# Seven block products in place of eight in four split-float32 matmuls, with a Prelu sign step and an Identity scale step

## The chip, the cores and the metric

The kernel runs on one core of a Trainium2 chip. The metric is device time in microseconds (us) of one execution. Before the change the median of three runs is 1053.89 us (1053.65 to 1054.04).

The core's engines run side by side and wait for each other by semaphores: TensorE multiplies (PE in the profile, its weight loads PEld), VectorE (DVE) and ScalarE (ACT) work element by element, SyncE (SP) issues the DMA transfers here, and GpSimd (POOL) does nothing of note.

## The reference

Attention with a sigmoid in place of a softmax, then two feed-forward blocks. Four large matmuls follow the attention; `w_in` is 768x2048 and `w_out` 2048x768 in each block.

```python
def _attn_ref(q, k, v):                        # q, k, v: (4, 12, 448, 64)
    scores = scale * np.matmul(q, k.transpose(0, 1, 3, 2)) - np.log(S)
    attn = 1.0 / (1.0 + np.exp(-scores))
    return np.matmul(attn, v).astype(np.float32)

def _moe_ref(x, w_in, w_out, s, b):            # x: (1792, 768)
    r = np.maximum(x @ w_in, 0.0)
    return ((s * (r * r) + b) @ w_out).astype(np.float32)

def _moe2_ref(x, w_in, w_out, alpha):
    h = x @ w_in
    return ((np.maximum(h, 0.0) + alpha * np.minimum(h, 0.0)) @ w_out).astype(np.float32)
```

The weights `w_in` and `w_out` arrive as float64, since numpy promotes them when they are scaled; the kernel gets their bits and makes float32 of them on the chip.

## The kernel before, in words

Activations are kept transposed, channels on the 128 partitions and tokens along the free dimension.

**Precision.** Every float32 operand of the four large matmuls is split in two: `hi`, rounded by a cast (ACT, L99 and L210, or DVE, L212), and `lo = x - hi` (DVE, L102 and L217). A product of two 128-wide blocks is then three matmuls into one PSUM bank, hi x lo, hi x hi and lo x hi (L411 to L413), each with a weight load of its own.

**Attention** (`emit_qk`, `emit_sig`, `emit_av`, `emit_x`). There are 84 steps. Step u issues the score matmuls of step u (L281) and the value matmuls of step u-2 (L307), both on 64x64 quarters of the array with 448 columns; ACT takes the sigmoid out of PSUM (L291), and a finished head pair is added up by ACT (L318) and DVE (L319). Beside this the 16 `w_in` units of block 1 are converted.

**The four matmuls** (`PASSES`, `in_mm`, `out_mm`). Three token groups, of 768, 512 and 512 tokens, go one after the other through block 1 and then through block 2, so there are six passes of 16 input units (`w_in`, six k blocks each) and 18 output units (`w_out`, three cuts for each of six output blocks). In the 768 group, `products` merges part of the work (L416) and does the rest as 256-column matmuls (L402). `in_evac` takes a unit's result from PSUM and applies relu, square, scale and offset (L437 to L454) or the two-sided slope (L461 to L472); `out_evac` copies the result and stores it.

**Weights.** A float64 unit is loaded (`load64`, L127), converted by `convert` in four steps (sign, L141 on ACT or L143 on DVE; exponent, L147; low bits, L152; joined, L155), stored as float32 (L165) and loaded again in later passes (`load32`, L174); `split_unit` makes hi and lo of it two units ahead of its use.

**Order.** Tile pools with two to four buffers for each kind of tile, PSUM in four double banks (`acc`, `av`); the order of the instructions on each engine is the order in which the Python loops issue them. The last unit of all is cut in two halves of 256 tokens (L494 to L507), so that the last copy and store are short.

Of the kernel before, what the change touches and what calls it, by code (L numbers as in the profile page):

```python
# [21 lines left out]
NWARM = 6  # L22

@with_exitstack
def tile_kernel(
# [19 lines left out]
    DM = NK * P  # L57
    NFC = w_in1.shape[0]
    QKSCALE = 1.0 / math.sqrt(D)
    WMAX = NK * P  # L60
    T2 = 2 * S

    REST = B * S - 3 * N5
    TG = N5 + REST
    TOK = [TG, N5, N5]
    TOK0 = [0, TG, TG + N5]
    NCUT = len(OUT_CUTS)
    PER = NFC + NK * NCUT

    def pool(name, bufs, **kw):  # L70
        return ctx.enter_context(tc.tile_pool(name=name, bufs=bufs, **kw))

    const = pool("const", 1)
    xp = pool("xp", 1)
    gp = pool("gp", 1)
    r64p = pool("r64", 2)
    cvp = pool("cvp", 1)
    wrawp = pool("wraw", 4)
    whlp = pool("whl", 4)
    tp = pool("tp", 4)  # L80
    ps = pool("ps", 2, space=PSUM)
    ps_av = pool("ps_av", 2, space=PSUM)
    dram = pool("dram", 1, space=DRAM)

    def acc_tile(name):
        return ps.tile([P, 2, 512], F32, tag="acc", name=name)

    def av_tile(name):
        return ps_av.tile([P, 2, 512], F32, tag="av", name=name)

    def t_tile(name):
        return tp.tile([P, TG], F32, tag="t", name=name)

    def g_tile(fc, name="g"):
        return gp.tile([P, WMAX + T2], F32, tag=f"g{fc}", name=f"{name}{fc}")

    def split(hi, lo, src, eng_hi):
        if eng_hi == "A":
            nc.scalar.copy(hi, src)  # L99
        else:  # L100
            nc.vector.tensor_copy(hi, src)
        nc.vector.tensor_tensor(out=lo, in0=src, in1=hi.bitcast(F32), op=ALU.subtract)  # L102

    bias_t = const.tile([P, 1], F32, name="bias_t")
    s_t = const.tile([P, 1], F32, name="s_t")
    b_t = const.tile([P, 1], F32, name="b_t")
    warm = const.tile([P, 1], F32, name="warm")
    al_t = const.tile([P, NFC], F32, name="al_t")
    nal_t = const.tile([P, NFC], F32, name="nal_t")


    units = []
    for wi, wo in ((w_in1, w_out1), (w_in2, w_out2)):
        for fc in range(NFC):
            units.append((wi[fc], WMAX))
# [519 lines left out]
```

## Time and profile before

| | before |
|---|---|
| median of 3 runs | 1053.89 us (1053.65 to 1054.04) |
| span of the profiled execution, first to last instruction | 1052.1 us |
| PE busy | 1047.9 us |
| DVE busy | 594.8 us |
| ACT busy | 448.5 us |
| moved by DMA | 173.17 MB |

The profiled execution's own time is its span, 1052.1 us, and what lies around it; 1.8 us separate it from the median of the runs. "Busy" of an engine is the share of the span in which at least one instruction of it runs. A matmul's duration in the trace is its way through the array, and the next one starts before it ends, so the pace of matmuls is read from their starts and not from their durations. In the chain of work that ended last, pieces have a start and a length, and the length of a run of matmuls is the time until the next piece.

### The profile page before, as it was taken

The page shows a single profiled execution, that of the slowest core. Times are in us where ns is not written, and L with a number is a line of the kernel's source. Part 1 is how long each engine was busy: PE and PEld are TensorE (multiplying, and loading weights), DVE is VectorE, ACT ScalarE, POOL GpSimd, SP SyncE. Part 2 cuts the span into 40 slices and gives each one's busy share as a digit, 9 for nine tenths or more (in the row PEclk, how much of TensorE's full clock was granted, in tenths as well). Part 3 has the DMA queues.
Part 4 walks back from the last instruction along what each step waited for, and adds up shares of the span by engine and source line. Part 5 has one row for each costly group of instructions (what it writes and reads, how often), then busy time and mean ns, then how long its engine had stood idle before and what let it go on. Part 6 is the DMA issues. An engine that isn't in the chain of part 4 may idle for free.

```text
span 1052.1 us, 14275 instructions
## 1 busy us (share of the span) xinstructions
PE 1047.9 (100%) x5631; PEld 818.3 (78%) x5631; DVE 594.8 (57%) x881; ACT 448.5 (43%) x625; POOL 0.2 (0%) x4
## 2 busy tenths in 40 slices
PE   9999999999999999999999999999999999999998
PEld 4333388888888888888888888888888888888887
DVE  4765456687643775447745366786616652266521
ACT  6777733444332554335534333443314432344321
POOL 0000000000000000000000000000000000000000
PEclk9999999999999999999999999999999999999999
DMA  7787660048762545764566512468523235323330
GB/s 276 274 268 248 244 249 1 27 140 262 250 225 93 195 138 203 270 207 136 183 220 207 187 61 60 120 187 291 201 93 105 89 122 170 130 90 98 116 117 31
DMA packets 62131, 173.17 MB, mean 165 GB/s; under 512 B 8048, under 2 KB 10736, under 8 KB 62064
## 3 DMA queue, kind: packets, MB, share of 16 engines
q1 hardware_dynamic: 62064, 172.27, 49.1%
q8 instruction: 44, 0.72, 0.3%
q14 instruction: 23, 0.19, 0.1%
HBM read 132.92 MB, written 39.32 MB: 164 GB/s over the span
## 4 chain that ended last, share of the span: by engine, by line
PE 100%; DVE 0%; issue 0%; DVEq 0%
PE hps L411 12%; PE hps L412 12%; PE hps L413 12%; PE ops L411 12%; PE ops L413 12%; PE ops L412 12%; PE sc L281 6%; PE av L307 6%; PE ops L416 4%; PE hps L416 4%; PE hps L402 2%; PE ops L402 2%; PE ops L494 0%; PE wp L345 0%; DVE o L503 0%
## 5 line engine op out<-in xcount | busy, mean ns | idle before, releaser
L102 DVE TENSOR_TENSOR whl<-wraw,whl 128x768 fp32r<-128x768 f32 (+1 forms) x188 | 167.8, 903 | 130.8 <-ACT whl L99 130.1
L411 PE MATMUL hps<-x,whl 128*128 128x512 f32 x576 | 224.4, 390 | 0.0
L412 PE MATMUL hps<-x,whl 128*128 128x512 f32 x576 | 224.3, 389 | 0.0
L413 PE MATMUL hps<-x,whl 128*128 128x512 f32 x576 | 224.1, 389 | 0.0
L411 PE MATMUL ops<-g,whl 128*128 128x512 f32 x571 | 222.4, 389 | 0.0
L412 PE MATMUL ops<-g,whl 128*128 128x512 f32 x571 | 222.3, 389 | 0.0
L413 PE MATMUL ops<-g,whl 128*128 128x512 f32 x571 | 222.1, 389 | 0.0
L99 ACT CAST whl<-wraw 128x768 fp32r<-128x768 f32 (+1 forms) x188 | 146.7, 792 | 40.8 <-PE ops L413 25.5
L411 PEld LDWEIGHTS hps<-x,whl 128*128 128x128 f32 x576 | 108.2, 188 | 22.7 <-issue 0.7
L413 PEld LDWEIGHTS hps<-x,whl 128*128 128x128 f32 x576 | 108.1, 188 | 22.6
L412 PEld LDWEIGHTS hps<-x,whl 128*128 128x128 f32 x576 | 108.2, 188 | 21.8
L413 PEld LDWEIGHTS ops<-g,whl 128*128 128x128 f32 x571 | 107.2, 188 | 22.4
L412 PEld LDWEIGHTS ops<-g,whl 128*128 128x128 f32 x571 | 107.2, 188 | 21.7
L411 PEld LDWEIGHTS ops<-g,whl 128*128 128x128 f32 x571 | 107.2, 188 | 21.7
L291 ACT ACTIVATE ga<-sc,bias_t 128x896 f32<-128x896 f32 x84 | 84.5, 1008 | 33.2 <-PE sc L281 31.5
L217 DVE TENSOR_TENSOR g<-t,g 128x512 fp32r<-128x512 f32 (+1 forms) x128 | 77.2, 624 | 31.8 <-ACT g L210 28.6
L437 ACT COPY o<-ops 128x512 f32<-128x512 f32 (+1 forms) x35 | 23.1, 661 | 149.0 <-PE ops L413 92.1
L281 PE MATMUL sc<-ga 64*64 64x448 f32 x672 | 78.3, 544 | 0.0
L307 PE MATMUL av<-ga,ga 64*64 64x448 f32 x672 | 77.1, 536 | 0.0
L147 DVE SCALAR_TENSOR_TENSOR cva<-r,cva 128x768 f32<-128x768 f32 (+1 forms) x68 | 61.7, 908 | 6.0 <-ACT cva L141 4.7
L210 ACT CAST g<-t 128x768 fp32r<-128x768 f32 x32 | 26.7, 836 | 85.8 <-DVE t L465 42.0
L217 DVE TENSOR_TENSOR x<-xr,x 128x512 fp32r<-128x512 f32 (+1 forms) x36 | 22.7, 645 | 59.0 <-ACT x L210 59.0
(53 smaller groups left out, 817.3 us busy)
## 6 DMA issues: line engine op xcount, KB each, us to landing
wraw<-w SPq DMA_DIRECT2D x104, 384.0 KB, 3.1
r<-in_w_in SPq DMA_DIRECT2D x32, 768.0 KB, 5.1
r<-in_w_out SPq DMA_DIRECT2D x24, 640.0 KB, 5.1
wraw<-w SPq DMA_DIRECT2D x48, 320.0 KB, 3.5
ga<-in_qk SPq DMA_DIRECT2D x23, 448.0 KB, 5.2
r<-in_w_out SPq DMA_DIRECT2D x12, 768.0 KB, 5.4
w<-wraw SPq DMA_DIRECT2D x24, 320.0 KB, 5.7
ga<-in_vt SPq DMA_DIRECT2D x24, 256.0 KB, 5.3
```

The lines of the kernel that those rows point to most:

```text
L99: nc.scalar.copy(hi, src)
L102: nc.vector.tensor_tensor(out=lo, in0=src, in1=hi.bitcast(F32), op=ALU.subtract)
L147: nc.vector.scalar_tensor_tensor(out=a.bitcast(F32), in0=hi.bitcast(F32), scalar=2.0**-112, in1=a.bitcast(F32), op0=ALU.mult, op1=ALU.max,)
L217: nc.vector.tensor_tensor(out=lo[:, a - o : e - o], in0=src[:, a - c0 : e - c0], in1=hi[:, a - c0 : e - c0].bitcast(F32), op=ALU.subtract,)
L281: nc.tensor.matmul(sc[h * D : (h + 1) * D, j, :S], kqt[q][rows, S + k0 : S + k0 + D], kqt[q][rows, :S], start=True, stop=True,)
L291: nc.scalar.activation(sg, sct.pop(u)[:, :, :S], AF.Sigmoid, bias=bias_t[:, 0:1], scale=QKSCALE)
L307: nc.tensor.matmul(avt[q][j * D : (j + 1) * D, h, :S], vtt[q][keys, j, c, :], sg[keys, j, :], start=first, stop=last,)
L402: nc.tensor.matmul(dst[:, N5:TG], lo, mv[:, 2 * N5 : N5 + TG], start=start and k == 0, stop=stop and k == n, skip_group_check=True,)
L411: nc.tensor.matmul(dst[:, :N5], hi, mv[:, N5 : 2 * N5], start=first and k == 0, stop=False)
L412: nc.tensor.matmul(dst[:, :N5], hi, mv[:, :N5], start=False, stop=False)
L413: nc.tensor.matmul(dst[:, :N5], lo, mv[:, N5 : 2 * N5], start=False, stop=end)
L416: nc.tensor.matmul(dst[:, N5 : 2 * N5], hi, mv[:, 2 * N5 :], start=first and not short_first and k == 0, stop=last and short_first and k == n,
```

## The change

Each of the four matmuls is cut into blocks of two by two and done with seven block products in place of eight (Strassen's method in Winograd's form: M1 to M7). The left operands are blocks of the weights or sums of them (A11, A12, A22, S1 to S4), the right ones blocks of the activations or differences, and the results are sums of products. In particular:

- Tokens are cut in four groups of 448 (S); two of them make one 2x2 cut. The six passes become four phases, (block, token half), each with an `in_phase` (eight pairs of unit rows x seven products x three k blocks x three matmuls) and an `out_phase` (seven products x three output pairs x eight k blocks x three matmuls). Every matmul has 448 columns.
- `quad` converts two float64 units at a time: ScalarE's Prelu does the sign and exponent steps in one instruction, two DVE steps do the low bits, four DVE additions make S1 to S4, and one DMA stores all seven left operands in DRAM. There are 34 quads, 20 in or right after the attention, 9 behind phase 0 and 5 behind phase 1 in program order. The buffers of the conversion (`R64` for two rows, `CVA`, `QUAD`) are single, and share their place with `XRAW[1]`.
- `unit` loads 1024 columns of left operands and splits them into a ring of three; 42 units in a phase.
- `make_x` forms the seven right operands of an input matmul (four differences, seven splits of 1344 columns); `prepare` does the same for an output matmul, one product ahead (four differences, seven splits of 3584 columns in three chunks).
- Results are added up while leaving PSUM (`pcopy` on ACT, `padd` and `psub` on DVE). M2, M4 and M7 accumulate in the bank that M1, M5 and M6 wrote, after that bank has been read.
- Scale and offset become an ACT Identity with scale and offset from SBUF; relu, square and Identity run on ACT for four blocks at a time.
- Nothing is issued as the loops run: every operation goes into a `Plan` with a written duration and what it reads and writes. `Plan.order` keeps PE's order, and picks for every other engine what can start first, then what is due first by the written durations. The kernel is issued in that order.
- PSUM is one tile of eight banks, SBUF is placed by hand.

```diff
...
-OUT_CUTS = [(0, 6), (6, 11), (11, 16)]
...
-PASSES = [(0, 0), (0, 1), (0, 2), (1, 0), (1, 1), (1, 2)]
-N5 = 512
...
+IN_ORDER = ["M1", "M5", "M6", "M2", "M7", "M4", "M3"]
+OUT_ORDER = ["M1", "M5", "M2", "M6", "M7", "M4", "M3"]
+LEFT = {"M1": "A11", "M2": "A12", "M3": "S4", "M4": "A22", "M5": "S1", "M6": "S2", "M7": "S3"}
+CHUNKS = [(0, 3), (3, 6), (6, 8)]
...
+class Plan:
...
+                if eng == "PE":
+                    i = pe[pe_at]
...
+                    pick = (max(f, est[i]), late[i], i)
+                else:
+                    pick = min((max(f, est[i]), late[i], i) for i in cand)
...
+    NSLOT = 37
+    NRING, NRAW, NTMP = 3, 2, 8
+    UNIT = 8 * P
+    WQ = KH * P
...
+    RING = [tensor(f"ring{i}", RING0 + i * 2 * UNIT, 2 * UNIT, F32R) for i in range(NRING)]
+    XRAW = {0: tensor("xraw0", RING0, 4 * XB), 1: tensor("xraw1", PROD, 4 * XB)}
+    R64 = [tensor(f"r64{i}", PROD + 4 * WQ * i, 4 * WQ) for i in range(2)]
+    CVA = tensor("cva", PROD + 8 * WQ, 2 * WQ)
+    QUAD = tensor("quad", PROD + 10 * WQ, 7 * WQ)
...
+    ps = psp.tile([P, 8, 512], F32, name="ps")
...
+    def quad(m, kind, k, c):
...
+        for row in range(2):
...
+            load(raw, src.bitcast(U32), 4 * n, (), cells(r64, 4 * n))
...
+                nc.scalar.activation(a, hi, AF.Prelu, scale=2.0**-112, alpha=-(2.0**32))
...
+                nc.vector.tensor_scalar(
+                    out=u, in0=lo, scalar1=2.0**-29, scalar2=7.0, op0=ALU.mult, op1=ALU.min
...
+                nc.vector.scalar_tensor_tensor(
+                    out=u, in0=a.bitcast(U32), scalar=3, in1=u,
...
+        tt("S1", "S3", "A22", ALU.add)
+        tt("S3", "A11", "S3", ALU.subtract)
+        tt("S2", "S1", "A11", ALU.subtract)
+        tt("S4", "A12", "S2", ALU.subtract)
...
+            "SP", dma_t(7 * n), lambda: nc.sync.dma_start(out=dst, in_=src),
...
+    def unit(m, kind, i):
...
+        raw, dst = RAW[g % NRAW], RING[g % NRING]
...
+        split(dst, dst + UNIT, raw, UNIT)
...
+    def make_x(par, raw):
...
+        half(0, p[0])
+        minus(p[0], p[1], p[0], XB)
+        half(1, p[0])
+        minus(p[0], p[3], p[0], XB)
+        half(2, p[0])
+        half(3, p[2])
+        minus(p[1], p[3], p[1], XB)
+        half(4, p[1])
+        minus(p[0], p[0], p[2], XB)
+        half(5, p[0])
+        half(6, p[3])
...
+    def mm_group(dst_bank, terms, first, last, more=False):
...
+                nc.tensor.matmul(d, wh_, ml_, start=first and k == 0, stop=False, **opt)
+                nc.tensor.matmul(d, wh_, mh_, start=False, stop=False, **opt)
+                nc.tensor.matmul(d, wl_, mh_, start=False, stop=last and k == n, **opt)
...
+    def nonlinear(m, par, mp, ps_):
...
+            add("ACT", act_t(n), lambda: nc.scalar.activation(h, h, AF.Relu), c, c)
+            add("ACT", act_t(n), lambda: nc.scalar.activation(h, h, AF.Square), c, c)
...
+                lambda: nc.scalar.activation(h, h, AF.Identity, bias=b_t, scale=s_t),
...
+    def in_phase(m, par):
...
+        for mp in range(NMP):
+            k0 = 4 * (mp % 2)
+            a, c, bb, e = k0, k0 + 1, k0 + 2, k0 + 3
+            to = {"M1": a, "M2": a, "M5": c, "M4": c, "M6": bb, "M7": bb, "M3": e}
+            second = {"M2", "M4", "M7"}
+            for i, x in enumerate(IN_ORDER):
...
+                if x == "M1":
+                    t = tmp()
+                    pcopy(t, a)
+                elif x == "M5":
+                    s_ = tmp()
+                    padd(s_, c, t)
...
+                elif x == "M6":
+                    q = tmp()
+                    padd(q, bb, s_)
+                elif x == "M2":
+                    pcopy(g_place(par, 0, mp), a)
...
+                elif x == "M7":
+                    padd(g_place(par, 3, mp), bb, s_)
...
+                elif x == "M4":
+                    psub(g_place(par, 2, mp), g_place(par, 3, mp), c)
...
+                else:
+                    padd(g_place(par, 1, mp), e, q)
...
+    def out_phase(m, g, par, middle):
...
+            "M1": (P1, None), "M5": (P1, (P2, P1)), "M2": (P3, None), "M6": (P1, (P4, P1)),
+            "M7": (P2, (P4, P2)), "M4": (P1, (P1, P3)), "M3": (P4, None),
...
+        prepare(0)
+        for i, x in enumerate(OUT_ORDER):
+            if i + 1 < 7:
+                prepare(i + 1)
+            if i in middle:
+                middle[i]()
+            for k in range(NDP):
+                unit(m, "out", i * NDP + k)
...
+    quads = []
+    for m in range(2):
+        quads += [(m, "in", k, 0) for k in range(NMP)]
+        quads += [(m, "out", k, c) for c in range(len(CHUNKS)) for k in range(NDP)]
...
+        if u == 4:
+            produce(20)
...
+    phases = [(0, 0), (0, 1), (1, 0), (1, 1)]
+    for n, (m, g) in enumerate(phases):
+        par = n % 2
+        in_phase(m, par)
...
+            def early(nxt=nxt):
+                load_x(*nxt)
+                make_x(1 - par, 1)
+
+            middle[6] = early
+        out_phase(m, g, par, middle)
+        if n == 0:
+            produce(9)
+        if n == 1:
+            produce(len(quads))
+    plan.emit()
```

## Rows read from the trace of the kernel before

**Rows 1.** Page, parts 1 and 2: PE's busy time; clock and DMA by slice.

```profile
PE 1047.9 (100%) x5631; PEld 818.3 (78%) x5631; DVE 594.8 (57%) x881; ACT 448.5 (43%) x625; POOL 0.2 (0%) x4
...
PEclk9999999999999999999999999999999999999999
DMA  7787660048762545764566512468523235323330
```

**Rows 2.** Page, part 4: the chain that ended last, by engine.

```profile
PE 100%; DVE 0%; issue 0%; DVEq 0%
```

**Rows 3.** Chain in order of time: start us, length us, what.

```profile
142.62 1.36 PE hps L416 x6
148.06 1.36 PE hps L416 x6
149.42 1.43 PE hps L402 x12
154.96 1.36 PE hps L416 x6
...
1045.40 3.60 PE ops L494 x30
```

**Rows 4.** Stretches: bounds: length, busy PE, PEld, DVE, ACT, POOL; clock, DMA share, GB/s.

```profile
0.00:131.40 131.40, 130.35 (x1393) 50.87 (x1393) 72.94 (x121) 97.09 (x111) 0.20 (x4) 1.00 0.75 262
...
330.50:461.00 130.50, 130.50 (x577) 108.06 (x576) 77.61 (x112) 57.14 (x88) 0.00 (x0) 1.00 0.58 195
...
660.00:710.00 50.00, 50.00 (x243) 42.29 (x242) 42.61 (x66) 23.27 (x31) 0.00 (x0) 1.00 0.54 160
```

**Rows 5.** Groups by form on PEld: busy us, mean ns | idle before.

```profile
L411 PEld LDWEIGHTS hps<-x,whl 128*128 128x128 f32 x576 | 108.2, 188 | 22.7 <-issue 0.7
...
L402 PEld LDWEIGHTS hps<-x,whl 128*128 128x128 f32 x192 | 25.1, 191 | 1.2
```

**Rows 6.** Groups by form on DVE: busy us, mean ns, idle before, releaser.

```profile
L102 DVE TENSOR_TENSOR whl<-wraw,whl 128x768 fp32r<-128x768 f32 x116 | 110.4, 952 | 30.3 <-ACT whl L99 30.2
...
L147 DVE SCALAR_TENSOR_TENSOR cva<-r,cva 128x768 f32<-128x768 f32 x44 | 42.0, 955 | 3.7 <-ACT cva L141 2.6
...
L319 DVE TENSOR_TENSOR xo<-av,xo 128x448 f32<-128x448 f32 x24 | 15.0, 624 | 39.9 <-ACT xo L318 39.9
...
L439 DVE TENSOR_TENSOR t<-hps,t 128x256 f32<-128x256 f32 x32 | 13.5, 423 | 34.5 <-ACT t L437 34.5
...
L152 DVE TENSOR_SCALAR cw<-r 128x768 uint32<-128x768 uint32 x16 | 8.9, 554 | 0.0
```

**Rows 7.** Groups by form on ACT, same columns.

```profile
L99 ACT CAST whl<-wraw 128x768 fp32r<-128x768 f32 x116 | 96.3, 831 | 14.0 <-PE ops L416 7.9 <-PE ops L413 4.3 <-DMA wraw<-w 1.7
L291 ACT ACTIVATE ga<-sc,bias_t 128x896 f32<-128x896 f32 x84 | 84.5, 1008 | 33.2 <-PE sc L281 31.5
...
L437 ACT COPY t<-hps 128x768 f32<-128x768 f32 x32 | 25.5, 798 | 43.6 <-PE hps L402 25.7 <-PE hps L416 16.2 <-issue 1.7
...
L141 ACT ACTIVATE cva<-r 128x768 f32<-128x768 f32 x28 | 25.5, 910 | 11.8 <-DVE wraw L155 6.5 <-DMA r<-in_w_out 5.2
...
L318 ACT COPY xo<-av 128x448 f32<-128x448 f32 x24 | 12.6, 524 | 0.5 <-PE av L307 0.5
...
L352 ACT ACT_TABLE_LOAD x1 | 1.3, 1283 | 0.7 <-PEq L625 0.7
```

**Rows 8.** Three stretches of 10 us, columns as in rows 4.

```profile
30.00:40.00 10.00, 10.00 (x112) 3.81 (x108) 5.70 (x10) 7.80 (x9) 0.00 (x0) 1.00 0.91 333
...
70.00:80.00 10.00, 10.00 (x112) 3.84 (x108) 5.61 (x10) 7.37 (x10) 0.00 (x0) 1.00 0.95 322
...
140.00:150.00 10.00, 10.00 (x49) 8.40 (x48) 6.61 (x11) 3.95 (x5) 0.00 (x0) 1.00 1.01 394
```

**Rows 9.** Page, part 6, DMA issues: count, KB each, us to landing.

```profile
wraw<-w SPq DMA_DIRECT2D x104, 384.0 KB, 3.1
r<-in_w_in SPq DMA_DIRECT2D x32, 768.0 KB, 5.1
```

More of the change, by code (lines that the diff above doesn't have):

```diff
@@ new lines, in tile_kernel, with split @@
+    n_unit = [0]
+    ring = {}
+    def unit(m, kind, i):
+        g = n_unit[0]
+        n_unit[0] += 1
+        raw, dst = RAW[g % NRAW], RING[g % NRING]
+        load(
+            sb(raw, UNIT), w32[m, kind][:, i * UNIT : (i + 1) * UNIT], UNIT,
+            [("d", m, kind, 8 * i + j) for j in range(8)], cells(raw, UNIT),
+        )
+        split(dst, dst + UNIT, raw, UNIT)
+        ring[m, kind, i] = dst
+    def split(hi, lo, src, n):
+        h, l, x = sb(hi, n), sb(lo, n), sb(src, n)
+        add("ACT", act_t(n), lambda: nc.scalar.copy(h, x), cells(src, n), cells(hi, n))
+        add(
+            "DVE", dve_t(n),
+            lambda: nc.vector.tensor_tensor(
+                out=l, in0=x, in1=h.bitcast(F32), op=ALU.subtract
+            ),
+            cells(src, n) + cells(hi, n), cells(lo, n),
+        )
@@ new lines, in minus, with slots @@
+    def minus(o, x, y, n):
+        o_, x_, y_ = sb(o, n), sb(x, n), sb(y, n)
+        add(
+            "DVE", dve_t(n),
+            lambda: nc.vector.tensor_tensor(out=o_, in0=x_, in1=y_, op=ALU.subtract),
+            cells(x, n) + cells(y, n), cells(o, n),
+        )
+    def slots(name, par, k, n, dtype=F32R):
+        if par:
+            k = NSLOT - k - n
+        return tensor(name, SLOTS + k * SLOT, n * SLOT, dtype)
+    X = [[slots(f"xo{p}{i}", p, 3 * i, 3) for i in range(7)] for p in range(2)]
@@ new lines, in make_x, with half, load_x @@
+    def make_x(par, raw):
+        p = [XRAW[raw] + i * XB for i in range(4)]
+        pl = X[par]
+        def half(i, src):
+            split(pl[i], pl[i] + XB, src, XB)
+        half(0, p[0])
[9 more added lines that the diff above has]
+        half(6, p[3])
+    def load_x(m, g):
+        for i in (0, 1, 3, 2):
+            to = XRAW[1] + i * XB
+            load(
+                sb(to, XB), x_dram[m, g][:, i * XB : (i + 1) * XB], XB,
+                [("x", m, g, i, j) for j in range(KH)], cells(to, XB),
+            )
@@ new lines, in pcopy, with f, padd @@
+    def pcopy(dst, k, func=None):
+        d = sb(dst, S)
+        def f():
+            if func is None:
+                nc.scalar.copy(d, bank(k))
+            else:
+                nc.scalar.activation(d, bank(k), func)
+        add("ACT", act_t(S, True), f, [("p", k)], cells(dst, S))
+    def padd(dst, k, other):
+        d, o = sb(dst, S), sb(other, S)
+        add(
+            "DVE", dve_t(S, True),
+            lambda: nc.vector.tensor_tensor(out=d, in0=bank(k), in1=o, op=ALU.add),
+            [("p", k)] + cells(other, S), cells(dst, S),
+        )
@@ L331, in flush_stores @@
-    def flush_stores():
-        for dst, t in stores:
-            nc.sync.dma_start(out=dst, in_=t)
-        stores.clear()
+        k = avt.pop(q)
+        kh, i = divmod(pr, KH)
+        o = (2 * kh + bb % 2) * XB + i * S
+        t = XRAW[0] + o if bb < 2 else tmp()
+        pcopy(t, k)
+        padd(t, k + 1, t)
+        if bb >= 2:
+            store(x_dram[0, 1][:, o : o + S], t, [("x", 0, 1, 2 * kh + bb % 2, i)])
+            free(t)
     ctx.enter_context(tc.manual_schedule())
-    idle = const.tile([P, P], F32, name="idle")
+    idle = sb(IDLE, P)
```

824 lines of the change are left out of this document (423 added, 401 removed).

## The prediction

> **What bounds the kernel now.** I read the page's busy times first, then the chain that ended last, then the chain piece by piece, then the stretches. PE is busy for 1047.9 of 1052.1 us at full clock in all forty slices [rows 1], and the chain is 100% PE [rows 2]. The reader should see that nothing but the number and pace of matmuls sets the time; DVE (594.8 us) and ACT (448.5 us) are covers with room in them. Busy PE time doesn't give the pace, so I take it from starts. In the 768 group 5.44 us lie between 142.62 and 148.06 [rows 3], for 24 matmuls of 512 columns: 0.2267 us each. A pass of 576 such matmuls agrees (130.5 us) [rows 4]. Thirty matmuls of 256 columns take 3.60 us [rows 3]: 0.120 us each.
>
> **The sum is built on three stretches.** Attention ends at 131.4 us [rows 4]. From there to 1049.0 (1045.40 + 3.60) [rows 3] PE works off 3840 matmuls of 512 and 384 of 256 columns. 3840 x 0.2267 + 384 x 0.120 = 916.6 us, and 131.4 + 916.6 = 1048.0, so the pace explains the trace to 1 us. The last 3.1 us are copy and store. The median lies 1.8 us above this execution's span; I add 1.8 again.
>
> **PE after.** A phase has 504 + 504 matmuls, four phases 4032, all of 448 columns. That form isn't in the trace. Between 256 and 512 columns the pace rises by 0.1067 us in 256, so 448 columns take 0.2267 - 64 x 0.000417 = 0.2000 us, and all of them 806.4 us instead of 916.6. From below: if nothing in a matmul is fixed, 0.2267 x 7/8 = 0.1984, 6.5 us less in all. From above: with 256-column matmuls at 0.1217 (12.34 us for two units at 142.62 and 154.96, less 48 x 0.2267, over 12) [rows 3], 0.2005, 2 us more; that a 448 column matmul costs as much as one of 512 is a rival below. I take 0.2000, the interpolation. The attention's matmuls are unchanged (131.4), and the tail still is one addition and a store of 128 rows (3.1). Floor: 131.4 + 806.4 + 3.1 + 1.8 = **942.7 us**.
> The row has 13.4 ns on each matmul above 512 columns at 2.4 GHz. The Trainium skill (TensorE: Matmul & The Clock Gate, Back-to-back issue gap) gives 2.5 ns of fixed cost, 189.2 ns at 448 columns; by it the products would take 763 us and the sum be 899. Its figure for 512 columns, 215.8 ns, differs from the measured 226.7, so I don't follow it.
>
> **DVE and ACT after.** DVE instructions on PSUM take 0.423 us (256) and 0.624 (448), so 0.155 + 1.047 ns a column, which gives 0.959 at 768 where SBUF rows have 0.952 [rows 6]. ACT takes 0.524 (448) and 0.798 (768), 0.831 from SBUF [rows 7], 0.86 ns a column.
> - Quads: two rows of 0.554 + 0.955, four additions of 0.557: 5.25 us DVE for 28, 3.9 for the six narrower: 170. Prelu replaces L141 and L147; L141's strided read took 0.910 [rows 7], I take the same: 59 us ACT. If Prelu were as fast as a plain cast it gains 0.08 each, 5 us of a covered engine.
> - Units: 168 x 1.227 = 206 DVE, 168 x 1.05 = 176 ACT.
> - `make_x`: 4 x 11 x 1.562 = 69 DVE, 37 ACT. `prepare`: 44 x 4.217 = 186 DVE, 100 ACT.
> - Results: 160 + 60 + 24 additions of 0.624 = 152 DVE, the slope step 35. ACT: copies 46, block 1's three steps 85, block 2's two relus 60. Identity with two operands from SBUF has no row; the sigmoid with one took 1.008 at 896 columns against 0.91 on the copies' line [rows 7], so 0.1 each, 0.2 for Identity (0 to 0.4, times 16, all on ACT).
>
> Together DVE 818 us and ACT 661 with the attention's 97 [rows 4]. Both stay below 943, but DVE's room is gone: phase 0 asks 206 us of it (in 51, out 81, `make_x` 17, quads 56) in 202 of PE, phase 1 196, phase 2 189, phase 3 150. In a full queue instructions start before the previous ends (DVE's groups add to 622 us where 594.8 are busy), so the true shares are 4 to 8% lower.
>
> **What can hold PE**, each from both sides:
> - Attention. ACT has 131.4 - 97.1 = 34 us free [rows 4]. Eight or nine quads bring 15, `make_x` 9, first units 3. A Prelu of 0.9 us in front of a sigmoid delays it by less than the two steps that PSUM covers, unless it waits for its DMA; behind it on ACT stand the sigmoids, and PE waits for them. 0 to 10 us, I take 3.
> - The first `out_phase`. It needs 17 quads. By its start at 131.4 + 100.8 = 232 us, DMA has to move q, k, v 17.3 MB, x 2.8, 17 quads 47.2 and 24 units 12.6: 79.8 MB. The fullest stretches moved 322 at share 0.95, 333 at 0.91 and 394 at 1.01 GB/s [rows 8], so 339 to 390 when full: 205 to 235 us. And `QUAD` is single: a quad's chain is 5.6 us of DVE and ACT and then a 1344 KB store of 3.5 to 4.1 us plus 2.0 (384 KB land in 3.1 [rows 9], 1.1 of it bytes), 11.4 us alone, some 14 beside the attention's loads, 14.5 beside a half busy DVE. That is 8.5 quads by 131.4, and the other 8.5 (three narrow ones at 10.5) by 242; the last is due at 236. 0 (at 11.4 each) to 25 us (at 17), I take 7.
> - Collisions on DVE. M7 adds to the bank that M6's result leaves by DVE, with only M2 between (nine matmuls, 1.8 us). If DVE has just begun a unit's split, 1.2 + 0.6 + a handover fill the 1.8: 32 times 0 to 0.4, and up to 12 more where phases 0 and 1 ask all of DVE. 0 to 25, I take 5.
> - Six changes between in and out. `make_x` needs 17 us of DVE within two products that leave 14, but later planes are due 1.8 us apart. 0 to 2 each, I take 3.
>
> What is removed beside PE's work (`convert`'s extra steps, the casts of six passes) was covered and gives nothing of its own; all transfers together grow from 173 MB to some 220, most of it unit loads, which after the first phase have room. Sum: 942.7 + 3 + 7 + 5 + 3 = **961 us** (960.7).
>
> **Rivals.**
> 1. The conversion holds PE. If a quad takes 17 us throughout, the attention loses its 10, the first `out_phase` 25, phase 1 with nine more quads 5, and the collisions stay: 942.7 + 40 + 5 = 988. For it: the single `QUAD`, the DMA share it asks for. Against: 394 GB/s were reached. Decides at some 14 us a quad.
> 2. DVE becomes the bound. From 131.4 on it has 741 us of work. Its highest share over 50 us so far is 42.6 of 50, 85% [rows 4]; at that share 872 us, and 131.4 + 872 + 4.9 = 1008. Against: it then had nothing more to do.
> 3. Prelu isn't in the sigmoid's table. One table load of 1.283 us served sigmoid, copy, relu and square [rows 7]; no row shows Prelu or Identity. If each Prelu among the sigmoids cost two loads, 34 x 1.283 = 44 us would join ACT's 124 in the attention: 37 over, 942.7 + 37 + 15 = 995. The Trainium skill (ScalarE: Activation LUTs, Table sets: the hidden batching unit) says cheap functions, relu, copy and identity among them, are in every set, and speaks of 2.7 us for a switch; the trace agrees for relu and copy, and no row shows Prelu.
> 4. The weight load sets the pace: 188 ns and a gap of 39 each [rows 5], so 0.2267 stays: 131.4 + 914 + 4.9 = 1050. Against: at 256 columns the load has 191 ns too and the pace is 0.120.
> 5. Slower than before. PSUM is one tile; if its results can't leave while PE writes another bank, each of 308 results (224 in, 84 out) stops PE for 0.624 us [rows 6]: 192 us, 1135. It decides from 178 of them on (111 us, the difference from floor to before). Nothing in the trace shows it; the banks alternate, which speaks against it.
>
> **How the numbers follow.** The forecast (943 to 975) gets 0.62, the rivals 0.16, 0.10, 0.03, 0.04 and 0.05. The range 943 to 1000 takes in the forecast with nearly all its bounds, rival 1 and rival 3: 0.81. About 0.2% is what a measurement of this kernel can tell from no change. Faster by more: 0.62 + 0.16 + 0.10 + 0.03 and half of rival 4, 0.93; within 0.2% the other half, 0.02; slower 0.05.
>
> **What would show it.** 448-column matmuls 0.200 us apart, at full clock. Attention's end near 134; a gap in PE, if any, at the first product of the first `out_phase`, ended by a unit whose load waited for a quad's store. In phases 0 to 2 DVE above 85% busy; M7's first matmul waiting for DVE in some row pairs. One table load. Wrong would be: a pace above 0.205, more than one table load, gaps at every product, or DVE with idle time while PE waits for it. A granted clock below 1.00 behind a gap would add to every stall above.

## The result and the profile after

The changed kernel takes 1024.46 us (median of four runs, 1022.11 to 1028.94) against 1053.79 for the one before: a ratio of 0.9727, 95% interval 0.9702 to 0.9752. It is faster by 29 us, where 93 were forecast: 961 was predicted, 943 to 1000 the range. The profiled execution has a span of 1020.9 us.

The page of the changed kernel, parts 1 and 2 (busy us, share and count; clock and DMA by slice), beside [rows 1]:

```profile
PE 972.0 (95%) x5424; PEld 828.7 (81%) x5424; DVE 762.6 (75%) x896; ACT 625.8 (61%) x675; POOL 0.2 (0%) x4
...
PEclk9999999998899999999999989998999999999999
DMA  8998999886776657776579568765444533333441
```

The chain that ended last, by engine, beside [rows 2]:

```profile
PE 62%; DVE 11%; DMA 6%; ACT 3%; issue 3%; SPq 0%; DVEq 0%; ACTq 0%
```

Before, the chain was 100% PE. Now PE stands still for 49 us, DVE and DMA have links in the chain, and the granted clock is below 0.9 in four slices. Where that lies is read from the stretches. The first row is the attention, then come the four phases, each an `in_phase` and an `out_phase` of 504 matmuls (columns as in [rows 4]):

```profile
0.00:134.00 134.00, 130.96 (x1392) 61.24 (x1392) 71.09 (x101) 115.02 (x134) 0.20 (x4) 1.00 0.90 323
134.00:248.10 114.10, 105.74 (x509) 95.55 (x505) 85.70 (x125) 81.05 (x82) 0.00 (x0) 0.98 0.86 296
248.10:369.40 121.30, 110.15 (x505) 98.54 (x506) 102.56 (x110) 61.25 (x65) 0.00 (x0) 0.93 0.66 226
369.40:481.70 112.30, 104.75 (x505) 95.61 (x504) 79.06 (x107) 77.71 (x75) 0.00 (x0) 0.98 0.74 254
481.70:591.70 110.00, 104.51 (x505) 95.71 (x505) 95.00 (x102) 59.25 (x63) 0.00 (x0) 0.98 0.69 227
591.70:710.20 118.50, 108.87 (x506) 98.46 (x505) 97.81 (x129) 70.02 (x84) 0.00 (x0) 0.94 0.70 236
710.20:812.40 102.20, 102.20 (x506) 94.64 (x506) 90.30 (x80) 56.89 (x57) 0.00 (x0) 1.00 0.43 131
812.40:915.10 102.70, 102.50 (x505) 94.50 (x504) 66.07 (x77) 58.21 (x69) 0.00 (x0) 1.00 0.36 108
915.10:1017.10 102.00, 102.00 (x505) 94.50 (x504) 74.35 (x69) 46.35 (x48) 0.00 (x0) 1.00 0.38 118
```

A stretch of 504 matmuls without gaps takes 102 us; the last three do. The first five take 114.1, 121.3, 112.3, 110.0 and 118.5, 66 us more in all: about 46 us of gaps over 0.6 us each, and some 16 us in matmuls at half clock behind them. All five are stretches in which weights are still converted. So there are two things to explain: the 66 us, and that even the quiet stretches take 102 us where 504 x 0.2000 = 100.8 were forecast.

### The profile page after: what moved, and what is told of

The parts are those of the page before. It is cut to its first block, busy times and chain, and to the rows that moved or that the text cites. A ratio compares the mean times of both kernels' runs of the same rounds, so it can differ in the third digit from the quotient of the medians.

```text
span 1020.9 us, 13856 instructions
## 1 busy us (share of the span) xinstructions
PE 972.0 (95%) x5424; PEld 828.7 (81%) x5424; DVE 762.6 (75%) x896; ACT 625.8 (61%) x675; POOL 0.2 (0%) x4
## 4 chain that ended last, share of the span: by engine, by line
PE 62%; DVE 11%; DMA 6%; ACT 3%; issue 3%; SPq 0%; DVEq 0%; ACTq 0%
PE ps L406 21%; PE ps L408 21%; PE ps L407 21%; DMA xraw<-x 3%; DVE ring L325 2%; DVE xo L325 2%; DVE gb L325 1%; DVE g L335 1%; DVE quad L284 1%; DMA r<-in_w_in 1%; DVE xraw L335 1%; DVE tmp L427 1%; ACT gb L322 1%; DVE quad L271 1%; DMA raw<-w0in 1%
## 5 line engine op out<-in xcount | busy, mean ns | idle before, releaser
L406 PE MATMUL ps<-xo,ring 128*128 128x448 f32 x672 | 250.9, 373 | 22.3 <-DVE tmp L427 18.7
L322 ACT CAST ring<-raw 128x1024 fp32r<-128x1024 f32 x168 | 175.3, 1047 | 154.6 <-PE ps L407 111.9
L406 PE MATMUL ps<-gb,ring 128*128 128x448 f32 x672 | 249.1, 371 | 10.7 <-ACT ring L322 7.5
L408 PE MATMUL ps<-gb,ring 128*128 128x448 f32 x672 | 249.0, 371 | 9.4 <-DVE ring L325 9.4
L407 PE MATMUL ps<-xo,ring 128*128 128x448 f32 x672 | 249.0, 370 | 0.0
L408 PE MATMUL ps<-xo,ring 128*128 128x448 f32 x672 | 248.7, 370 | 0.0
L407 PE MATMUL ps<-gb,ring 128*128 128x448 f32 x672 | 248.1, 369 | 0.0
L325 DVE TENSOR_TENSOR ring<-raw,ring 128x1024 fp32r<-128x1024 f32 x168 | 204.2, 1217 | 24.7 <-ACT ring L322 24.6
L406 PEld LDWEIGHTS ps<-xo,ring 128*128 128x128 f32 x672 | 128.6, 191 | 39.3 <-DVE tmp L427 23.1
L406 PEld LDWEIGHTS ps<-gb,ring 128*128 128x128 f32 x672 | 128.2, 191 | 23.4 <-ACT ring L322 10.6
L408 PEld LDWEIGHTS ps<-gb,ring 128*128 128x128 f32 x672 | 128.0, 190 | 22.1 <-DVE ring L325 11.5
L408 PEld LDWEIGHTS ps<-xo,ring 128*128 128x128 f32 x672 | 128.5, 191 | 10.7
L407 PEld LDWEIGHTS ps<-xo,ring 128*128 128x128 f32 x672 | 128.5, 191 | 10.3
L407 PEld LDWEIGHTS ps<-gb,ring 128*128 128x128 f32 x672 | 128.3, 191 | 10.4
L325 DVE TENSOR_TENSOR gb<-g,gb 128x1344 fp32r<-128x1344 f32 (+1 forms) x84 | 116.1, 1395 | 10.1 <-ACT gb L322 7.7
L322 ACT CAST gb<-g 128x1344 fp32r<-128x1344 f32 (+1 forms) x84 | 99.3, 1190 | 21.2 <-PE ps L408 14.5
L677 ACT ACTIVATE sg<-ps,bias 128x896 f32<-128x896 f32 x84 | 82.9, 1009 | 13.3 <-PE ps L661 12.6
L661 PE MATMUL ps<-kq 64*64 64x448 f32 x672 | 80.9, 542 | 2.0 <-ACT sg L677 2.0
```

Source lines behind the costliest of these rows:

```text
L322: add("ACT", act_t(n), lambda: nc.scalar.copy(h, x), cells(src, n), cells(hi, n))
L325: lambda: nc.vector.tensor_tensor(out=l, in0=x, in1=h.bitcast(F32), op=ALU.subtract),
L406: nc.tensor.matmul(d, wh_, ml_, start=first and k == 0, stop=False, **opt)
L407: nc.tensor.matmul(d, wh_, mh_, start=False, stop=False, **opt)
L408: nc.tensor.matmul(d, wl_, mh_, start=False, stop=last and k == n, **opt)
L661: nc.tensor.matmul(ps[h * D : (h + 1) * D, k + j, :S], a.ap[rows, S + k0 : S + k0 + D], a.ap[rows, :S], start=True, stop=True,)
```

## Experiments

**The names of the shared place.** `XRAW[1]`, the four planes that `load_x` brings for the next phase, shares its columns with `R64`, `CVA` and `QUAD`. The chain of the changed kernel late in the first `out_phase` shows quads waiting for planes (start us, length us, what):

```profile
310.71 1.03 DVE quad L266 x2
...
311.76 5.35 DMA xraw<-x
...
317.20 0.10 DVE quad L271
...
320.72 3.91 DMA xraw<-x
...
324.73 0.57 DVE quad L284
```

The plane in flight at 311.76 is the first, columns 0 to 1343 of the place. The quad's operation at 317.20 reads `CVA` and writes `QUAD`, columns 3072 to 6527. They have no column in common, and yet the one waits for the other, with all that is queued behind it on DVE. The planner's list knows columns and has no such wait. The wait comes in when the list is issued, where overlapping tensors seem to be treated as one. If so, giving each plane a name of its own takes it away:

```diff
-    XRAW = {0: tensor("xraw0", RING0, 4 * XB), 1: tensor("xraw1", PROD, 4 * XB)}
+    XRAW = {0: tensor("xraw0", RING0, 4 * XB), 1: [tensor(f"xraw1{i}", PROD + i * XB, XB) for i in range(4)]}
...
```

> Edit: the loaded X planes, which share their place with the conversion's tensors, are named as four tensors of 1344 columns instead of one of 5376; every address, every instruction and the order stay the same. Theory A (the waits at the changes of phase are put in for whole tensors that share any address, so that a quad's DVE operation waits for a plane that lies elsewhere, and all that is queued behind it on DVE, ACT and SP stands too): of the gaps of TensorE after 312 us, about 31 us in the trace of the changed kernel, some 20 to 25 go, and with them most of the half-clock stretches behind them (about 10 us): 990 to 1003 us, and the waits of `quad` for `xraw<-x` of 4 to 5.5 us are gone from the list of waits. Rival 1 (the waits are of the order of the transfers alone, the planes are late whatever their names): 1024, within 4 us. Rival 2 (DVE's queue is full there and sets the end): 1015 to 1024. The stretch before 312 us stays as it is by every theory.

Measured: **1000.0 us** (997.95 to 1002.19), 24.5 us less than the changed kernel, ratio to before 0.949 (0.947 to 0.9511). Addresses, operations and planned order are the same. What ended DVE's idle time before instructions on `quad` (releaser: us, times), first in the changed kernel, then in this one:

```profile
  DMA xraw<-x: 24.8, 6
  DMA w0in<-quad: 14.5, 6
  ACT cva L263: 12.0, 15
...
```

```profile
  ACT cva L263: 13.4, 15
  DMA w0in<-quad: 11.3, 6
  DMA r<-in_w_in: 6.9, 4
  DMA w0out<-quad: 6.0, 4
...
```

24.8 us of waiting for planes are gone, and no wait for planes is left in the list. The five long stretches become 113.8, 118.5, 105.2, 105.9 and 108.0 us: the third to fifth lose 21.7 us, the first two 3.1. The third to fifth in the kernel with four planes (columns as above):

```profile
363.40:468.60 105.20, 102.94 (x505) 94.41 (x505) 75.68 (x103) 75.59 (x73) 0.00 (x0) 1.00 0.76 260
468.60:574.50 105.90, 103.94 (x505) 95.91 (x505) 97.74 (x105) 61.70 (x66) 0.00 (x0) 0.98 0.74 244
574.50:682.50 108.00, 105.80 (x506) 95.74 (x505) 93.34 (x124) 67.88 (x82) 0.00 (x0) 0.98 0.74 245
```

The theory named the place and the price; both rivals are out.

**What holds phase 0: bytes, or additions?** Two edits of the changed kernel's list, each leaving every other instruction where it was:

```diff
-            load(raw, src.bitcast(U32), 4 * n, (), cells(r64, 4 * n))
+            w_ = 4 * n if m or row == 0 or (kind, k) == ("in", 0) else CELL
+            load(raw[:, :w_], src.bitcast(U32)[:, :w_], 4 * n, (), cells(r64, 4 * n))
```

> Edit: for the first layer's weights the second of a quad's two raw loads brings 64 of its 1536 (or 1024) words a partition; the arithmetic runs on what the buffer holds, so half of those weights is not read. It takes 12 MB of the 80 MB that are moved before 232 us away and leaves every instruction in its place. Theory A (the transfers hold the first two half-phases): the first in_phase and out_phase, 114.1 and 121.3 us in the changed kernel against 102.2 of one without gaps, become 20 to 28 us shorter together, and the time is 996 to 1005. Rival (DVE's chain of a quad and what is queued behind it holds them): under 5 us shorter, 1019 to 1024.

```diff
-                lambda: nc.vector.tensor_tensor(out=o_, in0=x_, in1=y_, op=op),
+                lambda: nc.vector.tensor_tensor(out=o_, in0=x_, in1=y_, op=op)
+                if m or (kind, k) == ("in", 0) else None,
```

> Edit: the four additions and subtractions that make S1 to S4 are left out of the first layer's quads (the first quad apart); DVE does 124 operations of 0.42 us less, 52 us, before 275 us, and each quad's chain is 1.7 us shorter; every transfer stays. Theory A (transfers hold the first two half-phases): 0 to 5 us shorter, 1019 to 1024. Rival (DVE holds them): 15 to 28 us shorter, 996 to 1009.

Measured: 1029.0 us (1023.78 to 1031.42) and 1029.2 (1025.6 to 1032.22), neither faster than 1024.5. (The second's expectation says 124 operations; the first layer has 16 quads beside the first one, so it was 64, some 34 us by their durations.) Both theories fell. The first edit did take the load off the DMA engines; in both fences the row is 134 to 250 us, first of the changed kernel, then of the first edit:

```profile
134.00:250.00 116.00, 106.84 (x510) 96.03 (x506) 87.60 (x129) 82.95 (x85) 0.00 (x0) 0.97 0.85 293
```

```profile
134.00:250.00 116.00, 106.87 (x504) 96.22 (x503) 90.51 (x132) 83.21 (x86) 0.00 (x0) 0.96 0.71 242
```

0.71 instead of 0.85 busy, and TensorE gets no further. The stores of the nine `w_out` quads run from 148.4 to 262.0 us in the changed kernel, from 145.2 to 259.2 with fewer bytes and from 146.0 to 260.1 without additions. An order fixed beforehand need not use time that is freed, so in these two edits a real cause could have stayed hidden. In the next four the list knows of each change.

**Order, or the one place of a quad.** Base is now the kernel with four planes (1000.0). The list's durations were off: by them the attention, which starts at 3.7 us, takes 168 groups of 0.81 us and ends at 140 us (134 measured).

```diff
-        return 0.1 + n * 4 * P / 330e3
+        return 0.1 + n * 4 * P / 390e3
...
-    MM = 0.2005
+    MM = 0.2028
...
-        add("PE", 0.81, f, r, pcells(k), PE_LAT)
+        add("PE", 0.765, f, r, pcells(k), PE_LAT)
...
-        add("PE", 0.81, f, r + w, w, PE_LAT)
+        add("PE", 0.765, f, r + w, w, PE_LAT)
```

> Base: the kernel with the four X planes. Edit: only durations in the planner's list: 390 instead of 330 GB/s for a transfer, 0.765 instead of 0.81 us for an attention group, 0.2028 instead of 0.2005 us for a matmul; no instruction changes, their order does. What holds the first two half-phases is neither the amount moved nor the additions (both were taken away without effect). Theory A (the order: Prelus and quad operations stand in ACT's and DVE's queues behind evictions that wait for TensorE, because the list was made for slower transfers): the gaps from 245 to 270 us (10.6 us, and 4.6 us at half clock) mostly go: 982 to 990. Theory B (the one place of the seven blocks: a quad's operations wait for the store of the quad before, 8.0 us from 40.80 to 48.73, then take 6.6 us themselves, 14.5 us a quad, 17 quads before the third product of the first out_phase can have its weights): the order can change little, 994 to 1003.

Measured: **998.7 us** (997.94 to 999.29). Better durations alone give nothing in all, as theory B had it, but they do move time: the first `in_phase` takes 106.9 us instead of 113.8, and starts at 138.7 instead of 131.2, since the attention is that much longer; the first `out_phase` takes 121.0 instead of 118.5.

```diff
-    QUAD = tensor("quad", PROD + 10 * WQ, 7 * WQ)
+    QUADS = [tensor("quad", PROD + 10 * WQ, 7 * WQ), tensor("quad2", SLOTS + 34 * SLOT, 7 * WQ)]
+    n_quad = [0]
...
+        n_quad[0] += 1
+        QUAD = QUADS[n_quad[0] % 2 if n_quad[0] < 14 else 0]
```

> Base: the kernel with the four X planes. Edit: the first 13 quads use two places in turn, the second in columns of the slots that are free during the attention; durations in the planner's list as they were, so the list still holds transfers at 330 GB/s for what sets the end. Theory B (one place): quads are stored every 10 to 11 us instead of 14.5 during the attention, the gaps from 245 to 270 us go even so: 980 to 990. Theory A (order): the list orders for slow transfers as before and the gaps stay or move into the first in_phase: 992 to 1005.

> Base: the kernel with the four X planes. Edits: two places for the first 13 quads, and the planner's durations. Theory B (one place): the first in_phase and out_phase come to 103 to 108 us each, the gaps from 245 to 270 us are gone, 972 to 985. Theory A (order): as with the durations alone, 982 to 990. If neither holds and it is the transfers after all (0.91 to 1.02 of the DMA engines from 130 to 180 us): 990 to 1003.

> Base: the kernel with new durations in the planner's list. Edit: the four additions that make S1 to S4 are left out of the first layer's quads (the first apart), and the list is told so. In the kernel with the old list leaving them out gave nothing. Theory B (one place: a quad costs its store and its own chain, one after the other): the cycle of 14.5 us is 1.7 us shorter and the gaps of the first out_phase are some 5 to 10 us less than with the new durations alone. Theory A (order): within 3 us of the new durations alone.

Measured: 993.5 us (992.23 to 996.61) with a second place, 991.4 (988.25 to 993.08) with a second place and the durations, 1000.0 (997.16 to 1001.25) without additions and with durations. Theory B gave lower times for all three. The first and third lie where theory A put them, the second where the transfers would; yet A had just failed with the durations. Two things can be read. During the attention quads came no faster with two places (in the kernel with both, eight stores from 27.3 to 131.2 us, 14.8 us apart in the mean, with one pause of 29.1 us). And the second place lay where the first `in_phase` evicts to, so evictions now waited for a quad's store. In the kernel with both, from 166 to 178 us (engine line, waited for: total us, times, longest):

```profile
ACT g L452 <- DMA w0out<-quad: 6.3, 1, 6.3
...
PE ps L409 <- DVE tmp L430: 5.7, 1, 5.7
```

So the experiment brought a wait of its own with it: the first `in_phase` took 113.7 us against 106.9 with the durations alone, while the first `out_phase` fell from 121.0 to 106.9. Leaving out the additions gave nothing even with a list that knows of it, and the trace shows where the time goes: the stores take longer instead. A store goes out at 176.8 us there, the next quad's first operation starts at 185.8 and its own store goes out at 191.8, which is 9.0 us of waiting and 5.9 of work where the kernel with additions has 7.1 and 7.5 (below). From issue to landing a wide `w_out` store takes 8.8 us (median) instead of 6.3 and a narrow one 6.4 instead of 4.1, and while the store of 176.8 is under way the DMA engines are 0.99 busy. So the transfers, too, have a part in a quad's time, and the `w_out` stores run from 148.2 to 257.4 us there, from 150.0 to 259.2 with the additions. What the one place means after the attention is seen in the kernel with new durations, from 195.2 to 211 us (engine, operation and count: ns min/median/max, first and last start us):

```profile
L302 SPq DMA_DIRECT2D w0out<-quad x2: 524/524/525, 195.3 to 209.9; - x2
L266 DVE TENSOR_SCALAR quad<-r x2: 554/557/560, 202.4 to 202.9; 128x768 uint32<-128x768 uint32 x2
L271 DVE SCALAR_TENSOR_TENSOR quad<-cva,quad x2: 948/950/951, 203.3 to 206.4; 128x768 uint32<-128x768 uint32 x2
```

A store goes out at 195.3, the next quad's first operation starts at 202.4 when it has landed, its own store goes out at 209.9: 7.1 us of waiting and 7.5 of work, in turn.

**Two places for all 17 quads.** The second place moved into four of the eight small buffers (`TMP`), which are then kept from other use until the first `out_phase`, and the buffer of the slope step (`NEG`), which only the second block uses:

```diff
+    QUADS = [QUAD, tensor("quad2", TMP[4].base, 7 * WQ)]
+    LATER = [TMP.pop() for _ in range(4)][::-1]
...
+        QUAD = QUADS[n_quad[0] % 2 if n_quad[0] < 18 else 0]
...
+        if n == 0:
+            TMP.extend(LATER)
         out_phase(m, g, par, middle)
```

> Base: the four X planes and the new durations (998.7 us). Edit: the second place lies in four of the eight small buffers and the buffer of the sign step instead of the free slots, so that all 17 quads of the first layer use two places in turn, not 13, and none of them in the columns that the first in_phase evicts into. During the attention the DMA engines are busy 0.95 of the time and a quad takes 14.5 us with one place or two; from 180 to 246 us they are busy 0.81, and there a quad's store of 6 to 7 us and its operations of 7 to 9 us stand one after the other. Theory B' (transfers hold the conversion during the attention, the one place after it): the last store of the 17 comes before 242 us instead of 259, the gaps between 250 and 272 us are gone, first in_phase and out_phase together 214 to 220 us instead of 228: 982 to 990. Theory C (transfers hold it throughout): the last store stays at 250 to 259 us, gaps move ahead: 990 to 1000.

> As the kernel before, with 360 GB/s in the planner's list, nearer to what the trace shows in full stretches (339 to 382 GB/s). Theory B': within 4 us of the kernel before, 980 to 990. Theory C: 990 to 1000. If the order by the planner's figure decides, the two kernels differ by over 5 us.

Measured: **980.4 us** (976.91 to 985.13), ratio to before 0.9291 (0.9269 to 0.9313), and 985.2 (984.17 to 991.64) with 360 GB/s in the list, 0.936 (0.933 to 0.939). From 180 to 246 us with one place, and then with two the same stretch, the first `in_phase` and the first `out_phase` (stretches as above):

```profile
180.00:246.00 66.00, 62.67 (x308) 57.33 (x307) 53.52 (x80) 52.50 (x51) 0.00 (x0) 1.00 0.81 274
```

```profile
180.00:246.00 66.00, 63.90 (x313) 58.13 (x311) 58.50 (x88) 54.69 (x55) 0.00 (x0) 1.00 0.95 338
...
136.70:240.80 104.10, 103.08 (x508) 94.42 (x505) 89.30 (x138) 78.60 (x78) 0.00 (x0) 1.00 0.97 355
240.80:350.00 109.20, 105.79 (x506) 95.79 (x505) 101.80 (x102) 65.57 (x68) 0.00 (x0) 0.98 0.64 220
```

The `w_out` stores of the kernel with one place, then of that with two:

```profile
L302 SPq DMA_DIRECT2D w0out<-quad x9: 524/525/604, 150.0 to 259.2; - x9
```

```profile
L307 SPq DMA_DIRECT2D w0out<-quad x9: 524/525/603, 152.7 to 237.7; - x9
```

The DMA engines, 0.81 busy while quads took turns with their stores, are 0.95 busy with two places; the last store comes at 237.7 instead of 259.2, and the first two stretches take 104.1 and 109.2 us instead of 106.9 and 121.0 (113.8 and 118.5 with the old durations). Theory B' is borne out: the store came within its bound, the stretches 0.7 us and the time 1.6 us below theirs. The two figures for the planner's transfers differ by 4.8 us, a little more than the 4 expected; their ranges overlap by 1 us, so I make nothing of it.

> Two places for all 17 quads, new durations; both raw loads of the first layer's quads (the first apart) bring 64 words a partition, so those weights aren't read, and the planner's list is told of it: 25 MB less. Theory B': during the attention a quad now takes 8 to 11 us instead of 14.5, the last of the 17 stores comes before 222 us, the time is 976 to 986, since only the changes of phase are left. Theory against it (ScalarE, 0.89 busy with the sigmoids, holds the conversion during the attention): 14 us a quad there as before, and the time of the kernel with two places.

Measured: 975.7 us (two runs, 971.86 and 979.57), not clearly less than with two places, whose range overlaps. The stores, and the stretch of the attention:

```profile
L308 SPq DMA_DIRECT2D w0out<-quad x9: 525/525/604, 127.4 to 202.1; - x9
L308 SPq DMA_DIRECT2D w0in<-quad x8: 326/334/408, 25.3 to 119.9; - x8
```

```profile
20.00:131.00 111.00, 109.78 (x1158) 44.10 (x1154) 76.64 (x107) 103.18 (x123) 0.00 (x0) 1.00 0.80 277
```

With 24 MB less the last of 17 stores comes at 202.1 us instead of 237.7, but most of that lead is won ahead of the first `w_out` store, which goes out at 127.4 instead of 152.7. Behind it a quad takes 9.3 us instead of 10.6, with the DMA engines 0.69 to 0.72 busy from 139 to 246 us. Half of a quad's bytes less makes it only an eighth faster, so the transfers are a part of what sets the pace once the place is doubled, and the rest isn't shown. Within the attention the expectation of 8 to 11 us a quad missed: eight stores in 94.6 us are 13.5 each, with ScalarE 0.93 and the DMA engines 0.80 busy. They don't come evenly: none goes out from 80.9 to 114.2 us, with ScalarE 0.96 and the DMA engines 0.81 busy, and in the kernel with two places none from 67.0 to 109.3, at 0.94 and 0.82. In these pauses the DMA engines have room; whether ScalarE or the list's order makes them is left open.

**What is left at the changes.** In the kernel with two places PE waits once for 3.4 us at the first product of the first `out_phase`, for the split of the last blocks. The last experiment asks for them later:

```diff
+            if i == 0:
+                parts = [(0, 0), (0, 1), (1, 0), (1, 1), (0, 2), (2, 0), (2, 1), (1, 2), (2, 2)]
...
```

> Base: two places for all 17 quads, new durations, four X planes (980.4 us). Edit: in the first product of an out_phase the third part of the blocks (two of eight) is taken later: parts 1, 2 of rows 0 and 1, then part 3 of row 0, and so on, so TensorE asks for it 3.6 us later. Theory A (what is left at the changes into an out_phase, 3.8 and 2.1 us with 3.4 us at half clock behind one, is the evictions, three ScalarE steps and split of the last row of blocks, which end too late for part 3): the gaps at 244 and 463 us are gone or under 0.5 us, 970 to 977. Rival (a weight unit that isn't there, or the ring of three units, holds the product): the gaps stay or come a product later, 978 to 984. By either theory 0.2067 instead of 0.2027 us for a matmul, in stretches that differ from run to run, moves the time by up to 4 us a 200 us.

Measured: 982.3 us (978.44 to 985.54), the same as without. What PE waited for from 230 to 262 us, first without the edit, then with it:

```profile
PE ps L411 <- DVE gb L330: 3.4, 1, 3.4
```

```profile
PE ps L411 <- DVE gb L330: 0.8, 1, 0.8
...
```

The gap at 244 us shrinks to 0.8 us, where at most 0.5 was expected, and that of the second `out_phase` (1.7 us) is gone. But the list has another order now, and from 540 to 572 us this stands in its trace:

```profile
ACT xo L327 <- DMA xraw<-x: 8.2, 1, 8.2
...
PE ps L411 <- DVE tmp L432: 6.3, 2, 4.0
```

A plane that lands late holds ScalarE's queue for 8.2 us and DVE's for 6.0, and PE waits 6.3 us for DVE, with 13.7 us at half clock behind it: the third `in_phase` takes 113.9 us where it took 108.7. The theory had the place of the gap right, but not the time: in the time there is no gain, since a new order brought a new wait.

**The pace by itself.** TensorE alone on zeros:

```diff
+    for n, step in ((512, 512), (448, 448), (448, 512), (384, 384), (256, 256)):
+        for g in range(24):
+            group(g % 6, n, step)
...
```

> Six stretches of TensorE alone on zeros, groups of 18 matmuls into one bank: 24 groups each of 512, of 448 columns, of 448 whose moving operands begin at multiples of 512, of 384 and of 256; then 36 groups of 448 with a ScalarE copy and a VectorE addition out of PSUM and SBUF copies beside them. Nothing of the reference is computed. Theory A (the pace is that of the shape: a cost by the column and a fixed part that is larger at 448 than on the line between 512 and 256): 0.2027 us in the second stretch and the same in the sixth. Rival (448 runs at 0.2000 us alone, and other engines or transfers beside it cost the 2.7 ns): 0.2000 in the second, 0.2027 in the sixth. If the third is at 0.2000 and the second not, it is the place of the operand.

One row from within each stretch, in that order (length, busy PE with the matmuls that run in it, some two of which began ahead of it; clock, DMA):

```profile
20.00:100.00 80.00, 80.00 (x355) 1.00 0.00 1
106.00:192.00 86.00, 86.00 (x426) 1.00 0.00 1
194.00:279.00 85.00, 85.00 (x421) 1.00 0.00 1
281.00:354.00 73.00, 73.00 (x423) 1.00 0.00 1
356.00:406.00 50.00, 50.00 (x419) 1.00 0.01 1
408.00:537.00 129.00, 129.00 (x638) 1.00 0.00 1
```

From the starts: 512 columns 0.2267 us (353 starts in 80 us), 448 columns 0.2027 in all three stretches (432 matmuls in 87.55 us), 384 columns 0.1734, 256 columns 0.1200. Theory A holds: 448 columns cost 0.2027 alone, with operands that begin at multiples of 448 or of 512, and with copies on ScalarE and additions on VectorE beside them. Transfers were not tried here, but in the changed kernel the last three stretches keep that pace with the DMA engines 0.36 to 0.43 busy. Three of the widths lie on one line, 13.3 ns above the columns at 2.4 GHz; 448 lies 2.7 ns above that line. The Trainium skill (TensorE: Matmul & The Clock Gate, Back-to-back issue gap) has N columns at 2.4 GHz and 2.5 ns of fixed cost for an isolated matmul; by it, as an estimate, 448 columns would take 0.189 us. The trace does not agree: 0.2027 at 448, and 13.3 ns of fixed cost at the other three widths.

## Why the prediction was wrong, step by step

**Six changes between in and out: "0 to 2 each, I take 3".** This is the step that failed. It priced only the operands' work on DVE. That the buffers of the conversion "share their place with `XRAW[1]`" stood in the description of the change and got no price at all: neither the real conflicts of columns nor what treating overlapping tensors as one makes of them. Naming the planes apart gave 24.5 us, 21.7 of them in the third to fifth stretch, waits and half clock together. No rival named it. That the waits come from the tensors' names and not from their columns is what the four names show, with addresses, operations and order unchanged; what the real conflicts of columns cost was not tried. With it gone the kernel would have ended at 1000, on the edge of the range.

**The first `out_phase`: "0 to 25, I take 7".** Right in mechanism, mis-sized. Its working gave 8.5 quads by 131.4 us and the 17th at 242; the trace has 8 stored by 132.4 and the 17th store at 262.0, since a wide quad took 15 us throughout and a narrow one 12, not 14.5 and 10.5. The stretch took 121.3 us, 19 more than a quiet one, and as the prediction said the gaps stand at its first products, before units: PE waits 13.4 us in seven places there for `ring`. The 7 follows from the working's 242 against 236, so what was mis-sized is the time of a quad. With two places for all 17 quads, and new durations, 19.6 us went (1000.0 to 980.4), 18.3 of them beyond what the durations alone gave. By stretches they came from the first `in_phase` (113.8 to 104.1) as much as from the first `out_phase` (118.5 to 109.2).

**Rival 1, the conversion holds PE (988).** In mechanism this came nearest (in time rivals 2 to 4 lay nearer, for reasons that did not hold): the conversion did hold PE, at 15 us a quad, just past the 14 from which it was said to decide. Its 17 us a quad weren't needed, and its time was passed because the waits of the first step came on top.

**PE's pace: 0.2000, bounds 0.1984 to 0.2005.** Mis-sized and outside its own bounds: 0.2027, 4032 x 0.0027 = 10.9 us. The interpolation between two widths assumed a line that the third width doesn't keep.

**Attention: 134 forecast, 134.0 measured** (131.4 before, [rows 4]). The mechanism is there, PE waits 2.0 us for sigmoids, but the exact hit is in part luck: the kernel with four planes, with the same operations in the same order, ends its attention at 131.2, with 0.2 us of such waits. The first `in_phase`, 12 us over a quiet stretch, was given nothing. PE waits there 4.0 us for results on DVE, 3.5 for a unit and 0.9 for a copy on ACT. It came down to 106.9 us with new durations, behind an attention 7.5 us longer, and to 104.1 with two places, so the order and the one place both have a part in it; with fewer bytes alone it did not.

**Collisions on DVE: 5.** With the planes apart PE waits 8.2 us in seven places for `tmp` from DVE. About right; the changed kernel's own 20.0 in ten places mix this with the step on the six changes.

**DVE and ACT.** 818 less 4 to 8% was forecast, 762.6 measured (6.8% less), ACT 661 against 625.8. Prelu and Identity, by form on ACT (busy us, mean ns), beside [rows 7]:

```profile
L263 ACT ACTIVATE cva<-r 128x768 f32<-128x768 f32 x56 | 51.1, 912 | 47.7 <-DVE quad L271 16.1 <-DMA r<-in_w_out 11.7 <-DMA r<-in_w_in 11.7
L453 ACT ACTIVATE g<-g,bc,sc 128x1792 f32<-128x1792 f32 x14 | 26.4, 1886 | 0.1
L450 ACT ACTIVATE g<-g 128x1792 f32<-128x1792 f32 x14 | 23.8, 1700 | 0.1
L737 ACT ACT_TABLE_LOAD x1 | 1.3, 1283 | 0.7 <-PEq L836 0.7
```

Prelu takes 912 ns where 910 was assumed, Identity 0.19 us more than Square where 0.2 was, and one table load serves all.

**Rivals 2 to 5.** DVE was 0.70 to 0.88 busy in the stretches of phases 0 to 2 and PE waited while it idled: not the bound. One table load: rival 3 is out. 0.2027 instead of 0.2267: rival 4 is out. The last three stretches have no gap: results leave PSUM beside matmuls, and rival 5, the slower ending, is out.

**"A granted clock below 1.00 behind a gap would add to every stall above"** came true and had no price: 0.93 to 0.98 in the five long stretches, about 16 of their 66 us.

Together: 942.7 as floor, 10.9 for the pace, 24.5 for the names, 19.6 for the place and the durations make 997.7 of 1024.5. The other 27 stay in the kernel with two places (980.4). Its profiled execution, 985.1 us, has 12.7 us of gaps, most at the changes, 4.5 at half clock behind them, some 5 in the longer attention, some 5 in a second pace (below), and the rest in small pieces. The forecast had given 18 us for all holds together. The four terms come from different runs, and their sum is an account and not a measurement.

## What to carry to other kernels

Where buffers lie over each other by hand, look in the trace for waits between parts that share no byte, and give each part a name of its own; a planner that counts columns doesn't see such waits. A chain of work and store through one place costs their sum each time; price it from the slowest row that the stretch will have, not from the row alone. Neither part is fixed: with less work the store took longer here (5.9 and 9.0 us instead of 7.5 and 7.1), and a second place helped where fewer additions did not. In an order fixed beforehand an edit that takes work away can show nothing, and a list that is told of it can give the gain back elsewhere, so read every stretch and not the time alone. A pace for a width that no row shows is worth a measurement: 2.7 ns a matmul were 11 us here.

## What the hardware showed beyond that

At a granted clock of 1.00 matmuls of 448 columns ran at one of two paces, 0.2027 or 0.2067 us, for 100 us and more at a time. In the kernel with two places, two stretches of 80 us without a gap (length, busy PE, clock, DMA):

```profile
260.00:340.00 80.00, 80.00 (x389) 1.00 0.72 251
700.00:780.00 80.00, 80.00 (x396) 1.00 0.44 144
```

Seven matmuls fewer in the first. Other executions have the slower pace elsewhere (the four planes from 610 to 840 us, the changed kernel hardly at all), with much or little DMA beside it, so it isn't tied to one stage or to the transfers. With fewer bytes and two places most of the products ran at it, some 12 us in all. It moves a run by up to 4 us in 200 and may be why runs of these kernels differ by up to 8 us where runs of the kernel before differ by 1 or 2; that isn't shown, since only one execution of each was profiled. What starts and ends it wasn't tried.
